# Copies of transposed q and k: reading PSUM in sequence and writing SBUF with a stride of three

## The chip, the cores and the metric

The kernel runs on one core of a Trainium2 chip. The metric is the device time of one execution in microseconds, as the median of several runs. Before the change it is 224.59 us (three runs, 224.47 to 225.51).

## The reference

Four batches with eight heads, 768 tokens and 64 columns per head go through attention in which each query sees the first 4 tokens and the last 128. The result, 3072 tokens of 512 columns, goes through a two-layer network with a swish of a beta per hidden column.

```python
scores = q @ k.T / sqrt(64)
keep = (pos[None, :] < 4) | ((rel >= 0) & (rel < 128))     # rel = query - key
a = softmax(where(keep, scores, -1e9))
x = (a @ v).reshape(3072, 512)
h = x @ w_in                                               # 512 -> 2048
out = (h * sigmoid(beta * h)) @ w_out                      # 2048 -> 512
```

## The kernel before, in words

Attention is cut into 32 units (`place`, L431): a unit `n` is a batch, a pair of heads and one half (384 tokens) of the sequence. Its q and k are loaded, cast to bf16 on GpSimd (L508; one on VectorE) and turned, so that the head's columns lie on the partitions: `qkT[pb]` holds, for each half, 384 columns of q and 384 of k. The scores (L560, L587, L624, L660) read `qkT` as both operands of TensorE's matmuls. Exponentials run on ScalarE (L563, L594, L631, L672), masks on VectorE (L605, L680) unless TensorE added them to the scores (L579), the product with v on TensorE (L703, L714), the division on VectorE (L723, L725). The result is turned back into `xT` (L742 and the copy L746, or a DMA). The network takes `xT` in eight stretches of 384 tokens: 16 groups of four matmuls with `w_in` (`hidden`, L765), a tanh on ScalarE (L773), a gate on VectorE (L788), and matmuls with `w_out` (`project`, L815) whose results leave through ScalarE and DMA.

Units 0 to 11 are turned by TensorE in `transpose_in` (L522); units 12 to 31 are turned by a DMA (L515), which the change doesn't touch. For the first twelve, the loads (`load_qk`, L444) put token 3p + c of the half onto partition p as its c-th piece, so that each descriptor covers three tokens. TensorE turns the three pieces c = 0, 1, 2 of q and of k one after the other into one bank of PSUM (L531): there the columns lie in the order (c, p), with c outside. `qkT` wants the tokens in their own order 3p + c, that is (p, c), with c inside. The copy from PSUM to `qkT` (`copy`, L536 to L541) puts them in order on its way.

The copies of units 2, 5, 6, 7, 8, 10 and 11 are one VectorE instruction over 768 elements, those of units 4 and 9 one of ScalarE (the table `TURN_IN`). Units 0, 1 and 3 are split into q on VectorE and k on ScalarE, 384 elements each, from two banks. That makes fifteen copies: seven and three on VectorE, two and three on ScalarE.

The order of work on each engine is fixed when the program is built: `Prog.order` (L178 on) places the operations by the cost that each is given and by their dependences, and `emit` writes one stream per engine with semaphore waits where another engine, or a VectorE or ScalarE result on the same engine, is needed. Each engine works through its stream strictly in order. The cost that `copy` gives the planner (L541) depends on the number of elements alone.

The start of the program runs units 0 to 3 one after the other, with filler matmuls on TensorE (`keep_busy`, L875). From then on TensorE alternates between `hidden` and `project` matmuls and the steps of later units, which the tables `EARLY` and `FIRST` put into slots.

The functions that the diff touches and what calls them:

Of the kernel before, what the change touches and what calls it, by code (L numbers as in the profile page):

```python
# [4 lines left out]
BF16 = mybir.dt.bfloat16  # L5
# [12 lines left out]
TT = 384  # L18
# [72 lines left out]
class Prog:  # L91
# [39 lines left out]
    def op(self, eng, fn, r=(), w=(), x=(), dma=None, busy=100.0, lag=None, behind=None,  # L131
           give=0.0, line=False, after=None):
        if self.group is not None and self.group.eng == eng:
            node = self.group
        else:
            node = Node(len(self.nodes), eng)
            self.nodes.append(node)
        events = []
        if after is not None:
            node.preds[after.id] = after  # L140
        if line:
            if self.line is not None:
                node.preds[self.line.id] = self.line
                self.line.soft.add(node.id)
            self.line = node

        def dep(ev, raw):
            if ev is None or ev[0] is node:
                return
            same = ev[0].eng == eng and ev[0].dma is None and dma is None  # L150
            node.preds[ev[0].id] = ev[0]
            if not same or (raw and eng != "pe"):
                events.append(ev)

        for t in r:
            dep(self.writer.get(t), True)
        for t in (*w, *x):
            dep(self.writer.get(t), False)
            for ev in self.readers.get(t, ()):
                dep(ev, False)  # L160
        if behind is not None:
            events.append((node, behind))
        me = (node, len(node.items))
        if dma is not None:
            self.dma_count[dma] = self.dma_count.get(dma, 0) + 16
            node.dma = (dma, self.dma_count[dma])
        node.items.append((fn, dma, events))
        node.busy += busy
        node.give = give
        node.lag = busy if lag is None else lag  # L170
        for t in r:
            self.readers.setdefault(t, []).append(me)
        for t in (*w, *x):
            self.writer[t] = me
            self.readers[t] = []
        return node
# [121 lines left out]
def bass_streamingllm_window__then__act_swish_beta_kernel(  # L298
# [21 lines left out]
    def sb(name, shape, dtype):  # L320
        ctx.append(nc.sbuf_tensor(name, list(shape), dtype))
        return ctx[-1].__enter__()
# [29 lines left out]
    qkT = [sb(f"qkT{z}", (128, 2, 2, TT), BF16) for z in range(4)]  # L352
# [17 lines left out]
    def pe(n):  # L370
        return {"busy": 2.5 + n / 2.4, "lag": 260.0}

    def act(n):
        return {"busy": 80.0 + 0.81 * n, "lag": 140.0}

    def dve(t):
        return {"busy": t, "lag": 140.0}
# [53 lines left out]
    def place(n):  # L431

        return n // 8, n % 4, n // 4 % 2, n % 4
# [88 lines left out]
    def transpose_in(n, bank=tr_ps, name_of="tr", eng="dve", apart=None):  # L522
        _, _, half, pb = place(n)
        z = n % NQK
        banks = [(bank, name_of, eng), apart or (bank, name_of, eng)]
        for which, name in enumerate("qk"):
            to, tag, _ = banks[which]
            with P.together("pe"):
                for c in range(3):
                    at = (3 * which + c) * 128  # L530
                    turned = op("pe", lambda e, which=which, c=c, at=at, to=to: nc.tensor.transpose(  # L531
                        to[:, :].bitcast(BF16)[:, at:at + 128],
                        qk16[z][:, which, c, :, :].rearrange("p h d -> p (h d)"), ident[:, :]),
                       r=[(name + "16", z), "ident"], w=[tag], **pe(128))

        def copy(eng, first, last, bank, tag, w):  # L536
            n = last - first
            dst = qkT[pb][:, half, first:last, :].rearrange("x w (p c) -> x w p c", c=3)
            src = bank[:, :].bitcast(BF16)[:, first * TT:last * TT].rearrange("x (w c p) -> x w p c", w=n, c=3)
            op(eng, lambda e: (e.copy if eng == "act" else e.tensor_copy)(dst, src), x=[tag], w=w,  # L540
               **(act(n * TT) if eng == "act" else dve(65.0 + n * 400.0)))  # L541

        if apart is None:
            copy(eng, 0, 2, bank, name_of, [("qT", pb, half), ("qkT", pb, half)])
        else:
            copy(eng, 0, 1, bank, name_of, [("qT", pb, half)])
            copy(apart[2], 1, 2, apart[0], apart[1], [("qkT", pb, half)])
        return turned
# [295 lines left out]
    for n in range(2, 4):  # L844
# [3 lines left out]
       w=["beta_stage"], dma="beta")  # L848
# [49 lines left out]
    for n in range(4):  # L898
# [19 lines left out]
       x=["acc0"], w=["beta"])  # L918
# [16 lines left out]
    for s in sorted(slots):  # L935
# [14 lines left out]
        for n, step in here:  # L950
            half = place(n)[2]
# [25 lines left out]
        if s in casts:  # L977
            n = casts[s]
# [20 lines left out]
        if s == 34:  # L999

            first = {0: (mask_a[:, :], MASK_A), 1: (mask_b[:, 128:512], MASK_B)}
# [78 lines left out]
```

## Time and profile before

| | |
|---|---|
| median of three runs | 224.59 us |
| the profiled execution | 225.3 us |
| its span, first to last instruction | 223.6 us |
| TensorE matmul busy | 217.0 us (97%) |
| VectorE busy | 128.9 us (58%), 257 instructions |
| ScalarE busy | 143.4 us (64%), 226 instructions |
| GpSimd busy | 72.1 us (32%) |
| first and last start of the changed copies | 5.3 and 52.7 us |

In the lines of the profile PE is TensorE's matmuls, PEld its weight loads, DVE VectorE, ACT ScalarE, POOL GpSimd and SP SyncE, with a q behind the name for the engine's own queue of instructions. L540 is line 540 of the kernel. Of a group of instructions the line shows its tiles, shapes and count, then total busy microseconds and mean nanoseconds of one, then the idle time of its engine ahead of it and what ended that. Tiles are named without their buffer numbers: `six` is the six banks of PSUM for scores and hidden columns, `acc` the two other banks. The ends of matmuls are modelled, so a full PE row doesn't mean that no matmul waited.

### The profile page before, as it was taken

To read this page: it belongs to the slowest core of one execution; us is meant where nothing else is said; L and a number is where in the kernel's file an instruction comes from. 1 tells how busy PE (TensorE), PEld (TensorE's weight loads), DVE (VectorE), ACT (ScalarE), POOL (GpSimd) and SP (SyncE) were. 2 spreads that over 40 slices of the span, in tenths; PEclk is the share of its full clock that TensorE was granted. 3 is DMA by queue.
4 is the path that set the end of the run, shared out by engine and by line. 5 is a ranking of instruction groups with operands and counts; after the bars stand their busy time and mean duration, and the time that the engine had idled before them with its cause. 6 is when DMAs were issued, how large, how long until landed. Compare 5 with 4: busy or idle time off the path is not lost.

```text
span 223.6 us, 4498 instructions
## 1 busy us (share of the span) xinstructions
PE 217.0 (97%) x1736; PEld 121.9 (55%) x1757; DVE 128.9 (58%) x257; ACT 143.4 (64%) x226; POOL 72.1 (32%) x149
## 2 busy tenths in 40 slices
PE   7998999999999999999999999999999999999995
PEld 4554556555545556555465556564656555555443
DVE  5474778898733367467194458574938466253300
ACT  2777996896256477666497568596767594465411
POOL 7666658987442213462210614600000000000000
PEclk9999999999999999999999999999999999999999
DMA  6999999997789999997995999622020202111022
GB/s 192 292 326 317 339 326 248 364 385 182 170 181 200 250 256 207 268 214 183 256 240 132 229 283 196 129 85 82 18 67 3 82 10 73 47 50 47 14 83 94
DMA packets 95437, 39.79 MB, mean 178 GB/s; under 512 B 81960, under 2 KB 88376, under 8 KB 95416
## 3 DMA queue, kind: packets, MB, share of 16 engines
q1 hardware_dynamic: 93760, 38.68, 68.1%
q10 hardware_dynamic: 1656, 0.83, 1.3%
q8 instruction: 14, 0.23, 0.5%
q14 instruction: 7, 0.06, 0.1%
HBM read 27.30 MB, written 6.29 MB: 150 GB/s over the span
## 4 chain that ended last, share of the span: by engine, by line
PE 86%; SPq 3%; DVE 2%; issue 2%; ACT 2%; POOL 2%; DMA 2%; POOLq 0%; DVEq 0%
PE acc L815 34%; PE six L765 31%; PE acc L765 5%; PE six L714 4%; PE six L660 3%; PE six L815 2%; SPq L457 2%; DMA v_stage<-in_v_dram 2%; PE six L587 1%; SPq L449 1%; PE six L703 1%; PE acc L796 1%; PE six L531 1%; PE six L560 1%; ACT th L773 1%
## 5 line engine op out<-in xcount | busy, mean ns | idle before, releaser
L815 PE MATMUL acc<-w_out,g 128*128 128x512 bf16 x332 | 84.0, 379 | 1.0 <-issue 0.3
L773 ACT ACTIVATE th<-six,beta_half 128x384 f32<-128x384 f32 x106 | 60.6, 583 | 30.0 <-PE six L765 24.1
L765 PE MATMUL six<-xT,w_in 128*128 128x384 bf16 x424 | 79.5, 326 | 0.1
L788 DVE SCALAR_TENSOR_TENSOR g<-th,six 128x384 bf16<-128x384 f32 x106 | 56.6, 550 | 26.5 <-ACT th L773 24.8
L765 PEld LDWEIGHTS six<-xT,w_in 128*128 128x128 bf16 x424 | 40.6, 98 | 29.9 <-issue 0.6
L815 PEld LDWEIGHTS acc<-w_out,g 128*128 128x128 bf16 x352 | 32.7, 98 | 33.7 <-issue 1.8
L680 DVE TENSOR_TENSOR E<-E,mask_all 128x1536 bf16<-128x1536 bf16 x20 | 19.4, 970 | 36.0 <-ACT E L672 26.6
L672 ACT ACTIVATE E<-six 128x1536 bf16<-128x1536 f32 x16 | 22.3, 1448 | 12.1 <-PE six L660 12.0
L508 POOL CAST qk<-q_stage 128x384 bf16<-128x384 f32 x32 | 16.5, 518 | 25.5 <-DMA q_stage<-in_q_dram 13.5
L511 POOL CAST v_aug<-v_stage 128x384 bf16<-128x384 f32 x32 | 17.1, 545 | 23.4 <-DMA v_stage<-in_v_dram 11.2
L594 ACT ACTIVATE E<-six 128x768 bf16<-128x768 f32 x24 | 19.3, 818 | 5.8 <-PE six L587 5.8
L508 POOL CAST qk<-k_stage 128x384 bf16<-128x384 f32 x31 | 17.3, 559 | 13.0 <-DMA k_stage<-in_k_dram 13.0
L823 ACT ACTIVATE out_sb<-acc 128x512 f32<-128x512 f32 x22 | 13.0, 595 | 10.5 <-PE acc L815 10.3
L765 PE MATMUL acc<-xT,w_in 128*128 128x384 bf16 x88 | 18.5, 327 | 0.7 <-DVE g L788 0.5
L714 PE MATMUL six<-v_aug,E 128*128 128x65 bf16 x384 | 19.0, 193 | 0.1
L714 PEld LDWEIGHTS six<-v_aug,E 128*128 128x128 bf16 x384 | 17.0, 97 | 3.6 <-issue 0.3
L725 DVE TENSOR_TENSOR o_norm<-six,rden 128x384 bf16<-128x384 f32 x32 | 17.8, 556 | 1.2
L788 DVE SCALAR_TENSOR_TENSOR g<-th,acc 128x384 bf16<-128x384 f32 x22 | 11.7, 548 | 5.0 <-ACT th L773 4.9
L773 ACT ACTIVATE th<-acc,beta_half 128x384 f32<-128x384 f32 x22 | 12.7, 591 | 2.6 <-PE acc L765 2.4
L563 ACT ACTIVATE E_sink<-six 128x384 bf16<-128x384 f32 x16 | 7.9, 497 | 5.7 <-PE six L560 5.7
L765 PEld LDWEIGHTS acc<-xT,w_in 128*128 128x128 bf16 x88 | 7.4, 98 | 5.6 <-DVE g L788 1.2
L703 PE MATMUL six<-v_sink,E_sink 128*128 128x130 bf16 x48 | 9.2, 220 | 0.1
(74 smaller groups left out, 155.6 us busy)
## 6 DMA issues: line engine op xcount, KB each, us to landing
out_dram<-out_sb SPq DMA_DIRECT2D x23, 256.0 KB, 2.6
wst<-in_moe_w_in_dram SPq DMA_DIRECT2D x8, 512.0 KB, 6.6
wst<-in_moe_w_out_dram SPq DMA_DIRECT2D x8, 512.0 KB, 8.5
q_stage<-in_q_dram SPq DMA_DIRECT2D x8, 384.0 KB, 3.7
k_stage<-in_k_dram SPq DMA_DIRECT2D x8, 384.0 KB, 4.0
v_stage<-in_v_dram SPq DMA_DIRECT2D x8, 384.0 KB, 4.4
v_stage<-in_v_dram SPq DMA_DIRECT2D x30, 96.0 KB, 4.7
q_stage<-in_q_dram SPq DMA_DIRECT2D x12, 192.0 KB, 5.3
```

Of the source, the lines that this page charges most:

```text
L508: op(eng, lambda e, x=x, name=name: e.tensor_copy(qk16[z][:, x, :, :, :], view(name)), r=[(name + "_stage", pb, half, hh) for hh in range( ...
L511: op("gp", lambda e: e.tensor_copy(v_aug[pb][:, 3 * half:3 * half + 3, :, 0:D], view("v")), r=[("v_stage", pb, half, hh) for hh in range(2 ...
L594: op("act", lambda e: e.activation(E[n % 2][:, c, :, 0:at], bank[:, 0:2, 0:at], AF.Exp, bias=0.0, scale=SCALE), x=[f"{name}0", f"{name}1"] ...
L672: op("act", lambda e, u=u, first=first: e.activation(E[u % 2][:, :, :, :].rearrange("p c h x -> p (c h x)"), six[:, first:first + 3, :].re ...
L680: op("dve", lambda e: e.tensor_tensor(both, both, mask_all[:, half, :].unsqueeze(1).to_broadcast([128, 2, 768]), ALU.mult), r=[("E", z, 0) ...
L714: last=(x == len(kbs) - 1): e.matmul(av_ps[:, at + hh * D1:at + hh * D1 + D1], E[z][:, c, h2, col:col + 128], v_aug[pb][:, kb, hh, :], sta ...
L725: op("dve", lambda e: e.tensor_tensor(o_norm[o][:, :, :, :].rearrange("p m h d -> p (m h) d"), src[:, :, 0:D], rden[z][:, :].unsqueeze(2). ...
L765: return op("pe", lambda e: e.matmul(bank, w_in16[:, c, m * 128:(m + 1) * 128], xT[:, c, T * TT:(T + 1) * TT], start=(c == 0), stop=(c == 3)),
L773: op("act", lambda e: e.activation(th[i % 3][:, :], bank, AF.Tanh, bias=0.0, scale=beta_half[:, m:m + 1]), x=[name], r=["beta"], w=[("th", ...
L788: op("dve", lambda e: e.scalar_tensor_tensor(g[T % 2][:, m, :], th[i % 3][:, :], 1.0, bank, ALU.add, ALU.mult), r=[("th", i % 3)], x=[name ...
L815: node = op("pe", lambda e: e.matmul(bank, g[T % 2][:, m, t * 128:(t + 1) * 128], w_out16[:, m, :], start=(m == 0), stop=(m == NM - 1)), r ...
L823: op("act", lambda e: e.activation(out_sb[z][:, :], bank, AF.Copy, bias=0.0, scale=0.5), x=[name], w=[("out_sb", z)], **act(NOUT))
```

## The change

The two views of the copy are built in another order of their dimensions. Before, both walk w (q, k), then p, then c: the write into `qkT` goes through memory in sequence, and the read from PSUM steps 128 elements (256 bytes) in its inner loop of three. After, both walk w, then c, then p: the read goes through PSUM in sequence, and the write steps three elements (6 bytes) in its inner loop of 128. The same elements land in the same places.

```diff
         def copy(eng, first, last, bank, tag, w):
             n = last - first
-            dst = qkT[pb][:, half, first:last, :].rearrange("x w (p c) -> x w p c", c=3)
-            src = bank[:, :].bitcast(BF16)[:, first * TT:last * TT].rearrange("x (w c p) -> x w p c", w=n, c=3)
+            dst = qkT[pb][:, half, first:last, :].rearrange("x w (p c) -> x w c p", c=3)
+            src = bank[:, :].bitcast(BF16)[:, first * TT:last * TT].rearrange("x (w c p) -> x w c p", w=n, c=3)
             op(eng, lambda e: (e.copy if eng == "act" else e.tensor_copy)(dst, src), x=[tag], w=w,
                **(act(n * TT) if eng == "act" else dve(65.0 + n * 400.0)))
```

## The prediction

> **What bounds the kernel now.** I read the chain that ended last first, then the stages, then the groups that hold the changed line, then each copy's surroundings in the timeline. The page gives the frame:
>
> ```profile
> span 223.6 us, 4498 instructions
> PE 86%; SPq 3%; DVE 2%; issue 2%; ACT 2%; POOL 2%; DMA 2%; POOLq 0%; DVEq 0%
> ```
>
> The stages (columns: time, then busy time and count of PE, PEld, DVE, ACT and POOL, granted clock, DMA share, GB/s) show where that chain is not PE:
>
> ```profile
> 4.00:18.00 14.00, 13.53 (x145) 7.81 (x143) 8.24 (x18) 8.75 (x14) 9.88 (x21) 1.00 1.07 313
> 18.00:36.00 18.00, 17.07 (x169) 9.45 (x170) 13.02 (x26) 15.84 (x29) 12.01 (x21) 1.00 1.04 317
> 36.00:56.00 20.00, 19.95 (x179) 11.62 (x178) 17.67 (x36) 16.30 (x29) 16.72 (x28) 1.00 0.94 298
> 56.00:223.60 167.60, 163.78 (x1237) 91.42 (x1255) 87.77 (x169) 101.07 (x153) 30.61 (x66) 1.00 0.61 138
> ```
>
> The clock is 1.00 throughout. TensorE, which works strictly in its written order, is nearly gapless from 18 us to the end, so microseconds that it loses early aren't won back: they come out at the end. All fifteen copies of the changed line lie in the first 54 us, the start (before 18 us) and the stretch in which VectorE and ScalarE are busy for 72% to 88% of the time. So the question is what one copy costs after the change, and which copies TensorE waits for.
>
> **The change part by part.** Nothing is added or moved: the same fifteen instructions on the same engines, with the same costs given to the planner, so the same order, waits and DMAs. What changes is the walk of each copy. Before, its inner loop reads PSUM at every 128th element (256 bytes) and writes SBUF in sequence; after, it reads in sequence and writes at every third element (6 bytes).
>
> Cost of a copy now, beside the copy L746, which is in sequence on both sides:
>
> ```profile
> L540 DVE COPY qkT<-six 128x768 bf16<-128x768 bf16 x7 | 6.7, 953 | 1.4 <-PE six L531 1.4
> L540 ACT COPY qkT<-six 128x768 bf16<-128x768 bf16 x2 | 1.6, 799 | 0.4 <-PE six L531 0.4
> L540 DVE COPY qkT<-acc 128x384 bf16<-128x384 bf16 x2 | 1.1, 558 | 1.4 <-PE acc L531 1.4
> L540 ACT COPY qkT<-six 128x384 bf16<-128x384 bf16 x2 | 1.0, 479 | 0.0
> L746 DVE COPY xT<-six 128x384 bf16<-128x384 bf16 x7 | 2.5, 353 | 1.9 <-PE six L742 1.9
> L746 ACT COPY xT<-six 128x384 bf16<-128x384 bf16 x2 | 1.0, 476 | 0.1
> ```
>
> VectorE: (953 - 558) / 384 = 1.03 ns an element, with 163 ns fixed. ScalarE: (799 - 479) / 384 = 0.83 ns, with 159 fixed. The ScalarE copy in sequence costs 476 against 479, so ScalarE pays nothing for the strided reads and has nothing to win. The VectorE copy in sequence takes 353: less the same 163 that is 190 / 384 = 0.49 ns, twice the rate. So there are 205 ns in a 384 copy and some 400 in a 768 copy to be won if a strided write, unlike a strided read, left the double rate in place.
>
> [...]
>
> I take no gain: the doubled row is the only one with both sides in sequence, and after the change the write side is as broken as the read side was.
>
> Is there a loss from the strided write? No copy of the trace has it. The nearest rows are VectorE's fills, two of which write one 2-byte element every 65 or 130 elements:
>
> ```profile
> L388 DVE MEMSET v_sink<- 128x1040 f32 x1 | 0.9, 925 | 0.1
> L388 DVE MEMSET ones<- 128x256 bf16 x1 | 0.3, 272 | 0.0
> L388 DVE MEMSET v_aug<- 128x12 bf16 x4 | 0.2, 68 | 0.0
> L388 DVE MEMSET v_sink<- 4x16 bf16 x2 | 0.1, 72 | 0.2
> L388 DVE MEMSET ones<- 32x32 f32 x1 | 0.1, 85 | 0.9 <-PEq L1062 0.9
> ```
>
> The three fills in sequence lie on a line: (925 - 272) / 784 and (272 - 85) / 224 are both 0.83 ns an element, with 58 fixed. It gives 58 + 12 × 0.83 = 68 for v_aug and 58 + 16 × 0.83 = 71 for v_sink; measured 68 and 72. Half a cycle more per element would have shown as 6 to 8 ns. So scattered 2-byte writes cost nothing visible there. The weakness: the runs are short, and the steps are 130 and 260 bytes, not 6, where neighbours fall into the same few words. The ends for the unknown price are therefore: below, the doubled rate (-400 ns for 768 elements, -205 for 384); above, one more cycle for every element, that is the rate halved as the row of L746 shows it doubled (+790 on VectorE and, at 0.83 ns, +640 on ScalarE for 768; half for 384). I take **zero**, by the fills.
>
> Next, what each copy is worth. Call d the growth of a VectorE copy of 768 and a that of ScalarE's; a copy of 384 grows by half. The timeline (start, duration, engine, and in brackets the idle time before it with what ended it):
>
> ```profile
> 11.25 0.10 PEld L587 LDWEIGHTS six<-qkT 64*128 64x128 bf16 x2 [0.29 <-DVE qkT L540]
> 18.14 0.50 PE L765 MATMUL acc<-xT,w_in 128*128 128x384 bf16 x2 [0.19 <-POOL w_in L493]
> 19.34 0.80 ACT L540 COPY qkT<-six 128x768 bf16<-128x768 bf16 x1 [0.40 <-PE six L531]
> 20.19 0.11 PEld L587 LDWEIGHTS six<-qkT 64*128 64x128 bf16 x4 [0.63 <-ACT qkT L540]
> 21.60 0.95 DVE L540 COPY qkT<-six 128x768 bf16<-128x768 bf16 x1
> 22.33 0.11 PEld L587 LDWEIGHTS six<-qkT 64*128 64x128 bf16 x4 [0.32 <-issue]
> 24.84 1.02 DVE L788 SCALAR_TENSOR_TENSOR g<-th,acc 128x384 bf16<-128x384 f32 x2 [1.37 <-ACT th L773]
> 27.35 0.54 DVE L788 SCALAR_TENSOR_TENSOR g<-th,acc 128x384 bf16<-128x384 f32 x1
> 28.01 0.11 PEld L587 LDWEIGHTS six<-qkT 64*128 64x128 bf16 x4 [0.32 <-DVE g L788]
> 29.65 0.96 DVE L540 COPY qkT<-six 128x768 bf16<-128x768 bf16 x1 [0.34 <-PE six L531]
> 34.78 1.09 PEld L765 LDWEIGHTS acc<-xT,w_in 128*128 128x128 bf16 x8 [0.37 <-DVE g L788]
> 39.45 0.96 DVE L540 COPY qkT<-six 128x768 bf16<-128x768 bf16 x1 [0.47 <-PE six L531]
> 40.64 0.10 PEld L587 LDWEIGHTS six<-qkT 64*128 64x128 bf16 x2 [0.32 <-DVE qkT L540]
> 46.54 0.60 ACT L773 ACTIVATE th<-acc,beta_half 128x384 f32<-128x384 f32 x1
> 47.29 0.10 PEld L587 LDWEIGHTS six<-qkT 64*128 64x128 bf16 x2 [0.32 <-ACT th L773]
> 55.46 0.36 DVE L746 COPY xT<-six 128x384 bf16<-128x384 bf16 x1 [0.59 <-PE six L742]
> ```
>
> - Units 0 to 3: k of units 0 and 1 on ScalarE and the whole of unit 2 (scores at 11.25 start when it ends) pass their growth along TensorE's start: a/2 + a/2 + d. But at 18.14 TensorE stands 0.19 us for a weight cast on GpSimd, which covers that much. q of units 0, 1 and 3 runs beside the other engine's copy.
> - Unit 4 (ScalarE, 19.34 to 20.14): the scores start 0.05 us later, so a passes whole.
> - Unit 5 (21.60): VectorE has 1.37 us to spare before 24.84; nothing passes.
> - Unit 6: the copy delays the gate at 27.35 to 27.89, and with it the scores at 28.01. The same 0.32 of idle also stands before scores that wait for nothing (22.33), so it is no wait for the copy: a released start takes 0.05, and 0.07 is to spare. d - 0.07 passes.
> - Unit 7 (29.65) begins VectorE's fullest stretch, whose end TensorE waits for at 34.78. d passes.
> - Unit 8 ends at 40.41, scores at 40.64: d - 0.18.
> - Unit 9 (ScalarE) delays the tanh that ends at 47.14, scores at 47.29: a - 0.10.
> - Units 10 and 11: VectorE has 0.59 to spare at 55.46: 2d - 0.59 if that is above zero.
>
> With d = a = 0 the sum is 0.0: the forecast is the median, **224.6 us** (the profiled execution took 225.3 for its span of 223.6; the sum is a difference, so it moves either figure alike, and I give it on the median of 224.59).
>
> **The rivals.**
>
> *Slower: the strided write costs part of a cycle for each element.* [...] d = 0.5 × 1.03 × 768 = 0.40, a = 0.32. Sum: start 0.16 + 0.16 + 0.40 - 0.19 = 0.53; unit 4 0.32; unit 6 0.33; unit 7 0.40; unit 8 0.22; unit 9 0.22; units 10 and 11 0.21; together 2.2: **226.8**. A whole cycle gives 1.24 + 0.64 + 0.72 + 0.79 + 0.61 + 0.54 + 0.99 = 5.5: 230.1. From a third of a cycle (d 0.26, a 0.21: 0.29 + 0.21 + 0.19 + 0.26 + 0.08 + 0.11 = 1.1) it leaves the half per cent. For it: no row shows steps this small. Against it: the fills, and the freedom from cost of the strided reads.
>
> [...]
>
> *Faster: reading PSUM in sequence is enough for the double rate on VectorE.* d = -0.40. TensorE then gains only where it truly stood for VectorE: 0.37 at 34.78; the start's gain ends at the weight cast of 18.14, and units 6 and 8 end in the fixed 0.32. That is **224.2**; were all three of units 6, 7 and 8 worth their 0.40, 1.2 and 223.4. For it: the row of L746. Against it: both of its sides are in sequence.
>
> *Nothing changes because the walk is the same to the engine.* The copies would show the same durations for another reason; same time as the forecast, counted with it.
>
> **How the numbers follow.** This kernel's three runs span 224.47 to 225.51, so about 0.5% (1.1 us) is what a measurement can tell from no change. Rates unchanged: 0.46, with a range of its own of 224.1 to 225.2. Strided write dearer: 0.45, of which 0.03 below a third of a cycle. Double rate: 0.09, of which 0.06 beyond half a per cent. So faster 0.06, same 0.46 + 0.03 + 0.03 = 0.52, slower 0.42. The range goes from 223.4, the best of the faster case, to 229.0, which takes in the dearer write up to about 0.8 of a cycle (d 0.63, a 0.51: 0.95 + 0.51 + 0.56 + 0.63 + 0.45 + 0.41 + 0.67 = 4.2, and as much as 0.2 for a slack that I saw too large); what is left out, a whole cycle, has under 0.1.
>
> **What would show it.** Right: VectorE's copies at 953 and 558 and ScalarE's at 799 and 479, within 10 ns. The slower rival: VectorE's 768 at 1.2 us or more, scores at 11, 20 and 40 us starting later, and TensorE from 56 us on moved as a whole. The faster one: 550. A split, with ScalarE dearer and VectorE not, would move units 4 and 9 alone. The step most open to error is the price of a write at a 6-byte step, taken from fills with far steps; the next is that time lost before 18 us is partly covered.

## The result, and the profile after

The changed kernel takes 227.69 us (227.53 to 227.85, four runs) against 224.57 (224.47 to 225.51): 1.0129 of the time before, with a 95% interval of 1.0101 to 1.0158. That is 3.1 us more; the two profiled spans differ by 2.5 (226.1 and 223.6). A second measurement gave 227.69 against 225.26: 1.0104 (1.0079 to 1.0129). Both intervals lie above 1, so the change makes the kernel slower. Of the runs below, one execution, the profiled one of the first run with VectorE alone, took 784 us; it stands outside the ratio, and its trace isn't read.

The frame of the page (it counts 21 instructions more since the trace of before lacks the records of 21 matmuls of L815; the programs have the same), and the groups of the changed line with two that were not changed:

```profile
span 226.1 us, 4519 instructions
PE 87%; DVE 8%; ACT 3%; issue 0%; DVEq 0%
```

```profile
L540 DVE COPY qkT<-six 128x768 bf16<-128x768 bf16 x7 | 10.1, 1446 | 1.4 <-PE six L531 1.4
L540 ACT COPY qkT<-six 128x768 bf16<-128x768 bf16 x2 | 2.9, 1457 | 0.8 <-PE six L531 0.8
L540 DVE COPY qkT<-acc 128x384 bf16<-128x384 bf16 x2 | 1.6, 800 | 1.6 <-PE acc L531 1.6
L540 ACT COPY qkT<-six 128x384 bf16<-128x384 bf16 x2 | 1.6, 812 | 0.0
L746 DVE COPY xT<-six 128x384 bf16<-128x384 bf16 x7 | 2.5, 354 | 1.4 <-PE six L742 1.4
L388 DVE MEMSET v_aug<- 128x12 bf16 x4 | 0.2, 68 | 0.0
```

All fifteen copies grew: VectorE's from 953 to 1446 ns and from 558 to 800, ScalarE's from 799 to 1457 and from 479 to 812, while L746, in sequence on both sides, stands at 354 (353 before), and the scattered fills of v_aug at 68. Per element VectorE now takes (1446 - 800) / 384 = 1.68 ns and ScalarE (1457 - 812) / 384 = 1.68: two engines with different rates before (1.03 and 0.83) have the same rate after. In the chain, VectorE's share went from 2% to 8%.

The stages after (same columns as before):

```profile
4.00:18.00 14.00, 12.87 (x139) 7.43 (x138) 8.56 (x17) 9.62 (x14) 10.25 (x21) 1.00 1.08 315
18.00:36.00 18.00, 16.68 (x169) 9.06 (x167) 13.16 (x24) 15.83 (x28) 13.32 (x23) 1.00 1.06 335
36.00:56.00 20.00, 19.11 (x171) 11.35 (x171) 18.62 (x34) 16.22 (x29) 16.14 (x27) 1.00 0.93 293
```

In these three stages, 52 us, PE's busy time fell by 0.66 + 0.39 + 0.84 = 1.9 us: TensorE stood that much longer. From 56 us on the work is only moved (the table of scores below). The copies and the waits behind them in the timeline:

```profile
12.15 0.10 PEld L587 LDWEIGHTS six<-qkT 64*128 64x128 bf16 x2 [0.78 <-DVE qkT L540]
19.87 1.44 ACT L540 COPY qkT<-six 128x768 bf16<-128x768 bf16 x1 [0.81 <-PE six L531]
21.36 0.11 PEld L587 LDWEIGHTS six<-qkT 64*128 64x128 bf16 x4 [1.26 <-ACT qkT L540]
29.16 0.11 PEld L587 LDWEIGHTS six<-qkT 64*128 64x128 bf16 x4 [0.32 <-DVE qkT L540]
33.97 1.53 DVE L605 TENSOR_TENSOR E<-E,mask_b 128x768 bf16<-128x768 bf16 x2
36.01 1.09 PEld L765 LDWEIGHTS acc<-xT,w_in 128*128 128x128 bf16 x8 [0.15 <-DVE g L788]
42.19 0.10 PEld L587 LDWEIGHTS six<-qkT 64*128 64x128 bf16 x2 [0.63 <-DVE qkT L540]
49.18 0.10 PEld L587 LDWEIGHTS six<-qkT 64*128 64x128 bf16 x2 [0.32 <-ACT qkT L540]
54.66 0.34 PEld L531 LDWEIGHTS six<-ident,qk 128*128 128x128 bf16 x6 [0.97 <-DVE qkT L540]
```

Against before, the scores at 12.15 (11.25) are 0.9 us late, those at 21.36 (20.19) 1.2, those at 42.19 (40.64) 1.6, those at 49.18 (47.29) 1.9. (How much of this a second trace of the same kernel would show is asked below.) The last line is new: unit 11's transposes stand 0.97 us for the copy of unit 10. Before, the same transposes waited for nothing, and the scores behind them started 2.5 us earlier than the 55.10 of after; VectorE's masks stand with them for a comparison below:

```profile
32.40 1.86 DVE L605 TENSOR_TENSOR E<-E,mask_b 128x768 bf16<-128x768 bf16 x2
51.92 0.54 PEld L531 LDWEIGHTS six<-ident,qk 128*128 128x128 bf16 x6
52.56 0.10 PEld L587 LDWEIGHTS six<-qkT 64*128 64x128 bf16 x2
```

### The profile page after: what moved, and what is told of

Read it like the earlier page. It is cut to its first block, busy times and chain, and to the rows that moved or that the text cites. A ratio compares the mean times of both kernels' runs of the same rounds, so it can differ in the third digit from the quotient of the medians.

```text
span 226.1 us, 4519 instructions
## 1 busy us (share of the span) xinstructions
PE 219.0 (97%) x1757; PEld 121.7 (54%) x1757; DVE 132.8 (59%) x257; ACT 145.2 (64%) x226; POOL 72.9 (32%) x149
## 4 chain that ended last, share of the span: by engine, by line
PE 87%; DVE 8%; ACT 3%; issue 0%; DVEq 0%
PE acc L815 34%; PE six L765 28%; PE six L714 5%; PE acc L765 3%; DVE qkT L540 3%; PE six L660 3%; DVE g L788 3%; PE six L579 2%; PE six L587 2%; PE six L815 2%; DVE E L605 1%; ACT E L594 1%; PE six L560 1%; PE six L531 1%; PE six L703 1%; PE acc L875 1%
## 5 line engine op out<-in xcount | busy, mean ns | idle before, releaser
L815 PE MATMUL acc<-w_out,g 128*128 128x512 bf16 x352 | 88.5, 379 | 0.0
L815 PEld LDWEIGHTS acc<-w_out,g 128*128 128x128 bf16 x352 | 32.7, 98 | 33.7 <-issue 1.8
L508 POOL CAST qk<-q_stage 128x384 bf16<-128x384 f32 x32 | 17.0, 533 | 29.4 <-DMA q_stage<-in_q_dram 14.9
L511 POOL CAST v_aug<-v_stage 128x384 bf16<-128x384 f32 x32 | 17.7, 565 | 25.8 <-DMA v_stage<-in_v_dram 12.6
L508 POOL CAST qk<-k_stage 128x384 bf16<-128x384 f32 x31 | 15.6, 506 | 11.9 <-DMA k_stage<-in_k_dram 11.7
L540 DVE COPY qkT<-six 128x768 bf16<-128x768 bf16 (+1 forms) x8 | 10.9, 1366 | 1.9 <-PE six L531 1.9
```

The lines of the kernel that those rows point to most:

```text
L508: op(eng, lambda e, x=x, name=name: e.tensor_copy(qk16[z][:, x, :, :, :], view(name)), r=[(name + "_stage", pb, half, hh) for hh in range( ...
L511: op("gp", lambda e: e.tensor_copy(v_aug[pb][:, 3 * half:3 * half + 3, :, 0:D], view("v")), r=[("v_stage", pb, half, hh) for hh in range(2 ...
L815: node = op("pe", lambda e: e.matmul(bank, g[T % 2][:, m, t * 128:(t + 1) * 128], w_out16[:, m, :], start=(m == 0), stop=(m == NM - 1)), r ...
```

## Experiments

Ratios are to runs of before on the same chip. Where a kernel has the copies in both forms, the two walks stand behind a condition:

```diff
+            walk = "x w c p" if <condition> else "x w p c"
-            dst = ...rearrange("x w (p c) -> x w p c", c=3)
-            src = ...rearrange("x (w c p) -> x w p c", w=n, c=3)
+            dst = ...rearrange("x w (p c) -> " + walk, c=3)
+            src = ...rearrange("x (w c p) -> " + walk, w=n, c=3)
```

### What a strided write costs: the first probe

Single copies and fills behind the last work of the kernel of before. The diff is a summary: in the kernel each is a line of its own, and a dozen more (short runs, 32-bit copies of ScalarE, strided reads of SBUF) are left out here.

```diff
+    for s in (1, 2, 3, 4, 6, 8, 12, 16, 32):      # 16-bit, hb: a bank of PSUM; fx: SBUF
+        e.tensor_copy(fx[:, 0:384 * s:s], hb[:, 0:384])
+    for s in (1, 2, 3, 4, 16):                    # 32-bit
+        e.tensor_copy(fx32[:, 0:384 * s:s], h32[:, 0:384])
+    e.tensor_copy(fx[:, 0:1152].rearrange("p (a b) -> p a b", b=6)[:, :, 0:2], ...)
+    for n, s in ((384, 1), (384, 3), (12, 65), (188, 65)):
+        e.memset(fx[:, 0:n * s:s], 0.0)
+    for s in (1, 2, 3, 4, 8, 16):                 # ScalarE, 16-bit
+        e.copy(fw[:, 0:384 * s:s], ab[:, 0:384])
```

> The kernel of before with some forty single copies and fills put behind its last work, PSUM to SBUF, 128 partitions, each with another step of the write; their results are used by nothing, so the time of the whole means nothing and only the durations count. Theory A (an element that is written with a step of over one word costs a second slot of about 0.83 ns, whatever the engine and the step): 16-bit copies of 384 at 558 (VectorE, step 1 at 353 in pairs) and at 803 for every step from 3 up, ScalarE 479 and 805; a fill of 384 at step 3 slower than at step 1 by 320 ns, the fill of 188 at step 65 by 157, and short runs of 12 hardly. Theory B (only steps that keep neighbours in the same few words cost; far steps are free, as the fills at steps 65 and 130 seemed to show): 803 at steps 2 to 4, back to 558 at steps of 16 and 32, and the fill at step 65 at 58 + 188 x 0.83 = 214 ns. Theory C (the engine's walk over three encoded dimensions costs, not the step): a single run at step 3 takes 558, as none of these copies has a second dimension.

VectorE, in the timeline: 16-bit steps 1, 2, 3, 4, 6, 8 and 32, then 32-bit steps 3, 4 and 16, then 192 pairs of adjacent 16-bit elements every 6 elements, then two 16-bit fills, 384 at step 3 and 188 at step 65:

```profile
211.68 0.36 DVE L1052 COPY xT<-six 128x384 bf16<-128x384 bf16 x1
212.07 0.59 DVE L1053 COPY xT<-six 128x384 bf16<-128x384 bf16 x1
212.69 0.80 DVE L1054 COPY xT<-six 128x384 bf16<-128x384 bf16 x1
213.53 1.01 DVE L1055 COPY xT<-six 128x384 bf16<-128x384 bf16 x1
214.58 1.45 DVE L1056 COPY xT<-six 128x384 bf16<-128x384 bf16 x1
216.06 1.88 DVE L1057 COPY xT<-six 128x384 bf16<-128x384 bf16 x1
221.67 1.82 DVE L1060 COPY xT<-six 128x384 bf16<-128x384 bf16 x1
226.61 0.66 DVE L1067 COPY xT<-six 128x384 f32<-128x384 f32 x1
227.30 0.84 DVE L1068 COPY xT<-six 128x384 f32<-128x384 f32 x1
228.17 0.81 DVE L1069 COPY xT<-six 128x384 f32<-128x384 f32 x1
229.01 0.41 DVE L1070 COPY xT<-six 128x384 bf16<-128x384 bf16 x1
230.54 0.38 DVE L1073 MEMSET xT<- 128x384 bf16 x1 [0.39 <-DVE xT L1072]
231.85 0.21 DVE L1075 MEMSET xT<- 128x188 bf16 x1 [0.75 <-DVE xT L1074]
```

ScalarE, 16-bit steps 1, 3 and 8:

```profile
224.61 0.48 ACT L1077 COPY w_in<-acc 128x384 bf16<-128x384 bf16 x1 [6.65 <-DVE acc L1051]
225.74 0.80 ACT L1079 COPY w_in<-acc 128x384 bf16<-128x384 bf16 x1
228.35 1.87 ACT L1081 COPY w_in<-acc 128x384 bf16<-128x384 bf16 x1
```

None of the three theories holds. The cost isn't one extra slot (A): it grows with the step. It isn't confined to near steps (B): it grows up to step 8 and then stays. And it isn't the encoded shape (C): single runs pay. Less the 0.16 us fixed, an element takes 1.12, 1.67, 2.21, 3.36 and 4.48 ns at steps 2, 3, 4, 6 and 8, and 4.3 at 32. A step of 8 elements is 16 bytes, and 4.48 times 2/8, 3/8, 4/8 and 6/8 is 1.12, 1.68, 2.24 and 3.36. So the times are those of about 4.5 ns for each 16-byte line that the copy writes in pieces, on either engine (ScalarE takes 1.67 ns an element at step 3 and 4.45 at step 8); at step 3 that is 1.68 ns an element, the rate of the changed copies. On VectorE, 32-bit elements at steps of 3, 4 and 16 take 1.30, 1.77 and 1.69, about 1.75 for a line: less than half. The pairs come to (0.41 - 0.16) / 192 = 1.30 a pair, the price of a 32-bit element at the same 12 bytes. The fills pay nothing: 384 at step 3 take 0.38, which is 58 + 384 × 0.83 = 377 ns.

### Which side of it is slow: the second probe

Seven of its eighteen copies, fills and products:

```diff
+    e.tensor_copy(fx[:, 0:1152:3], fx[:, 4000:4384])                        # from SBUF
+    e.tensor_copy(fx[:, 0:1152:3], h32[:, 0:384])                           # fp32 to 16 bits
+    e.tensor_scalar(fx32[:, 0:1152:3], h32[:, 0:384], 0.5, None, ALU.mult)  # fp32 to fp32
+    e.tensor_tensor(fx[:, 0:1152:3], fx[:, 4000:4384], fx[:, 5000:5384], ALU.mult)
+    e.memset(fx[:, 0:3072:8], 1.0)
+    e.copy(fw[:, 0:1152:3], fw[:, 4000:4384])                               # ScalarE, from SBUF
+    e.copy(fw32[:, 0:1152:3], ab[:, 0:384])                                 # ScalarE, 16 bits to fp32
```

> Single copies and fills behind the last work of the kernel of before, as in the first probe, whose result was: 16-bit copies pay by 16-byte lines (4.4 to 4.5 ns for each line that they touch, from step 2 to step 8, and flat beyond), 32-bit copies 1.7 ns for a line, fills nothing. Theory (an element of half a 4-byte word costs extra when it is written alone, whatever the source): 384 elements at step 3 take 0.80 from SBUF, from fp32 and with a multiplication too, at step 8 1.9; a 32-bit write of 16-bit sources at step 3 takes 0.66; fills of ones at step 8 0.38 like fills of zeros. Rival (it is the way from PSUM that is slow): from SBUF 0.56. Rival (it is the 16-bit source): from fp32 0.66. Rival for the fills (zeros are a special case): ones at step 8 1.8.

In the order of the diff:

```profile
213.30 0.49 DVE L1052 COPY xT<-xT 128x384 bf16<-128x384 bf16 x1
214.89 0.80 DVE L1054 CAST xT<-six 128x384 bf16<-128x384 f32 x1
216.56 0.68 DVE L1056 TENSOR_SCALAR xT<-six 128x384 f32<-128x384 f32 x1
217.27 0.80 DVE L1057 TENSOR_TENSOR xT<-xT 128x384 bf16<-128x384 bf16 x1
221.76 0.38 DVE L1060 MEMSET xT<- 128x384 bf16 x1 [1.46 <-issue]
224.40 0.83 ACT L1066 COPY w_in<-w_in 128x384 bf16<-128x384 bf16 x1 [4.81 <-DVE acc L1051]
228.74 0.66 ACT L1069 CAST w_in<-acc 128x384 f32<-128x384 bf16 x1 [0.46 <-ACT out_sb L802]
```

The product of two SBUF tensors, written at step 3, takes 0.80 like the copy from PSUM, and ScalarE from SBUF 0.83: the source doesn't matter. Nor does its type: fp32 to 16 bits 0.80, 16 bits to fp32 0.66. What counts in these runs is the size of the element that is written alone. VectorE's copy within SBUF is the exception: 0.49 at step 3 and, in the same trace, 1.02 at step 8. Less the 0.16 fixed these are 0.86 and 2.24 ns an element, half the price at both steps; why is open. Fills of ones at step 8 are as free as those of zeros (0.38 both); why fills are spared wasn't found.

### The parts: VectorE alone, ScalarE alone, and the whole again

Conditions `eng == "dve"` and `eng == "act"`.

> Only the ten VectorE copies write with the step of three; the five ScalarE copies stay as before; the order of work is that of before. Theory (the strided write costs each engine on its own account, and the end moves through the scores that wait): VectorE's copies at 1446 and 803 ns, ScalarE's at 799 and 479, and by the prediction's sum with d = 0.49 and a = 0: start 0.49 - 0.19 = 0.30, unit 6 0.42, unit 7 0.49, unit 8 0.31, units 10 and 11 0.39: 1.9 us above before. Rival (ScalarE's copies carry the loss, since its growth per copy is the larger): under 0.8 us. Rival (each loss is hidden unless the other is there too): under 0.8 us here and in the next run.

> Only the five ScalarE copies write with the step of three. Theory: ScalarE's copies at 1457 and 805 ns, VectorE's at 953 and 558, and by the prediction's sum with a = 0.66 and d = 0: start 0.33 + 0.33 - 0.19 = 0.47, unit 4 0.66, unit 9 0.56: 1.7 us above before; together with the run before it 3.6, where the full change showed 3.1. Rival (VectorE carries all of it): under 0.5 us.

> The whole change once more, so that it and its parts stand beside the same runs of before on one chip. Theory: between 1.0% and 1.6% above before (2.3 to 3.5 us), with VectorE's copies at 1.44 and 0.80 us and ScalarE's at 1.46 and 0.81. Rival (the first measurement was a chance of its chip): about 0.75%, the sum of its two parts as measured (0.54% and 0.21%).

> Only the VectorE copies, again, since the trace of the first run of this part can't be read. Theory, mended by the run with ScalarE alone (whose delay from unit 4 vanished under VectorE's full stretch before 34.8 us): the two parts don't add up, because each engine's delay is covered while the other engine is the late one; VectorE alone 1.2 us (0.54%) as before, with most of it behind unit 7: from 30 to 41 us the scores late by 0.5 to 0.9, at 55 us by 1.2 to 1.6. Rival (the parts add up): 1.9 us.

Measured: VectorE alone 1.0054 (1.0034 to 1.0074) and, again, 1.0058 (1.0021 to 1.0096); ScalarE alone 1.0021 (0.9999 to 1.0043); the whole 1.0104 (1.0079 to 1.0129). With VectorE alone the scores are 0.75 late at 41.39 and 1.4 at 53.99, as expected. In microseconds the parts and the whole are 1.2 to 1.3, 0.5 and 2.3, where the sum had 1.9, 1.7 and 3.8: each part is smaller than its terms, ScalarE's by most. 0.58% and 0.21% make 0.79%, just the lower end of the whole's interval; whether the parts add up isn't settled.

The expectation of the second run with VectorE alone says that ScalarE's delay from unit 4 vanishes under VectorE's full stretch before 34.8 us. The traces don't show that. With ScalarE alone, unit 4's scores are 0.55 late (20.74 for 20.19), and those of unit 8 only 0.10 (40.74 for 40.64). But VectorE's two masks in between, the first of these lines, are 0.34 shorter than the 1.86 of before, and the same two masks are as short in the second line, from the run with units 10 and 11 alone, whose copies up to there are those of before:

```profile
32.84 1.52 DVE L606 TENSOR_TENSOR E<-E,mask_b 128x768 bf16<-128x768 bf16 x2
32.14 1.53 DVE L608 TENSOR_TENSOR E<-E,mask_b 128x768 bf16<-128x768 bf16 x2
```

With ScalarE alone the masks start 0.44 late and end 0.10 late. So the delay went in masks that differ from one execution to the next, and it is no cover that the change can count on. How much of ScalarE's delay reaches the end is known by the times alone: 0 to 1.0 us by the interval, where the sum had 1.7.

The starts of the weight loads of some scores in the traces:

| scores of | before | after | whole, again | VectorE alone | ScalarE alone | units 0-3 | units 10, 11 | all but 10 |
|---|---|---|---|---|---|---|---|---|
| unit 4 | 20.19 | 21.36 | 20.67 | 20.59 | 20.74 | 20.58 | 19.93 | 21.69 |
| unit 8 | 40.64 | 42.19 | 41.63 | 41.39 | 40.74 | 40.65 | 40.05 | 42.51 |
| unit 9 | 47.29 | 49.18 | 48.62 | 48.45 | 47.48 | 47.30 | 47.04 | 49.51 |
| unit 10 | 52.56 | 55.10 | 54.54 | 53.99 | 52.88 | 52.70 | 52.60 | 54.93 |
| units 16, 17 | 92.81 | 95.37 | 94.79 | 94.23 | 93.13 | 92.94 | 92.85 | 95.23 |

Each column is one execution, and the first rows vary from one to the next. The two probes run the work of before up to 200 us, so they are two more traces of it: their scores of unit 4 start at 20.02 and at 21.71, where before has 20.19. The first row by itself therefore shows no effect of a change. A step down a column varies less: from unit 4 to unit 8 the probes take 20.19 and 20.24, before 20.45, the whole change 20.83 and 20.96.

From unit 10 to units 16 and 17 every column takes 40.24 to 40.27, but for 40.30 in the last: what is lost by 55 us stays lost, and nothing is lost after it. From unit 9 to unit 10 it is 5.27 before (5.27 and 5.31 in the probes), 5.92 in both traces of the whole change, 5.54 with VectorE's copies alone and 5.40 with ScalarE's.

### Units 0 to 3, units 10 and 11, and all but unit 10

Conditions on the unit: `n < 4`, `n in (10, 11)`, `n != 10`.

> Only the copies of units 0 to 3 (four of VectorE, three of ScalarE) write with the step of three. The prediction's term: 0.33 + 0.33 + 0.49 - 0.19 = 0.96 us. Theory now: the scores of units 1 to 3 start 0.4 to 0.9 late as in the changed kernel, but the weights that come by DMA until 32 us, and VectorE's slack before 34.8, cover most: 0 to 0.4 us at the end. Rival (nothing covers): 0.9.

> Only the copies of units 10 and 11 (both VectorE, 768) write with the step of three. The prediction's term: 2 x 0.49 - 0.59 = 0.39 us, by VectorE's slack at 55.46. Theory from the changed kernel's trace: unit 11's transposes go into the bank that unit 10's copy reads, so they wait for it, and 0.3 to 0.7 us is lost there, before VectorE's slack counts at all; the wait of the transposes for the copy should show at 52 us. Rival (hidden): none.

> The whole change, but unit 10's copy as before (0.95 us). Theory: in the changed kernel TensorE stands about a microsecond before unit 11's transposes, for unit 10's copy to leave the bank; with that copy short the wait falls below 0.6 and the end is 0.3 to 0.5 us earlier than the whole change, so 0.85% above before where the whole change had 1.04%. Rival (VectorE's load behind it sets the time, as the prediction had it): the wait goes but the end stays.

Units 0 to 3: 1.0011 (0.9994 to 1.0028), 0.25 us and at most 0.6, where the term was 0.96. In its trace the scores of unit 3 are 0.75 late (15.06 for 14.31), those of unit 4 0.39, those of unit 8 0.01. So most of what the first units lose doesn't reach the end. Where it is given back isn't shown: the masks at 32 us took 1.43 here and 1.86 before, and the time from unit 3's scores to unit 4's is 5.52, as with units 10 and 11 alone, where nothing up to there is changed.

Units 10 and 11: 1.0017 (0.9993 to 1.0042), 0.4 us, no more than the edge of the measurement; the trace has 0.29 from unit 9 to unit 10 (5.56 against 5.27). The wait of the transposes shows, but not all of it comes from the longer copy: with ScalarE alone and with units 0 to 3 alone, where unit 10's copy is as before, the same transposes stand 0.44 and 0.13 is lost.

```profile
52.16 0.34 PEld L531 LDWEIGHTS six<-ident,qk 128*128 128x128 bf16 x6 [0.60 <-DVE qkT L543]
```

All but unit 10: 1.0081 (1.0050 to 1.0113) beside the whole's 1.0104; the times can't tell the two apart, the trace can. From unit 9 to unit 10 it takes 5.42 instead of 5.92, with the masks there as long as in the whole change, so half a microsecond of the whole change's loss is that one copy. Its wait has halved, not gone:

```profile
54.49 0.34 PEld L531 LDWEIGHTS six<-ident,qk 128*128 128x128 bf16 x6 [0.47 <-DVE qkT L543]
```

### Both sides in sequence

```diff
-            dst = ...rearrange("x w (p c) -> x w p c", c=3)
-            src = ...rearrange("x (w c p) -> x w p c", w=n, c=3)
+            dst = qkT[pb][:, half, first:last, :]
+            src = ...rearrange("x (w y) -> x w y", w=n)
```

> All fifteen copies read PSUM in sequence and write SBUF in sequence, so the columns of q and k stay in the order in which they were turned: the keys and queries are permuted against the masks, and only the time means something. Theory (the rate falls through the step of the written or read side, and VectorE has its double rate only where both are in sequence): VectorE's copies at 553 and 353 ns, ScalarE's unchanged at 799 and 479; the end gains 0.4 us (the one true wait at 34.78) to 1.2 us. Rival (before's copies are held by something else than the step): 953 and 558 ns and no gain.

0.9969 (0.9952 to 0.9987): 0.7 us gained, between the 0.4 and the 1.2. The rate is the doubled one:

```profile
L540 DVE COPY qkT<-six 128x768 bf16<-128x768 bf16 x7 | 3.9, 551 | 1.4 <-PE six L531 1.4
L540 DVE COPY qkT<-acc 128x384 bf16<-128x384 bf16 x2 | 0.7, 359 | 2.2 <-PE acc L531 2.2
```

### Two ways on: the true costs in the plan, and tokens in order

```diff
-  **(act(n * TT) if eng == "act" else dve(65.0 + n * 400.0))
+  **(act(n * TT * 2) if eng == "act" else dve(65.0 + n * 645.0))
```

> The whole change, with the copies' measured costs given to the planner (VectorE 65 + 645 per 384 elements, ScalarE twice its cost per element), so that the order of work is laid out anew around the longer copies. Theory (the loss is time on the path, not a bad order): at most a third of the loss comes back: 0.7% to 1.1% above before. Rival (the order was the loss): within 0.3% of before.

The second way, cut short (the old body of `load_qk` goes, and the copy is that of the run in sequence):

```diff
     def load_qk(n, name, queue="sp"):
+        for hh in range(2):
+            load_head(n, name, hh, queue)
```

> Units 0 to 11 load their q and k with tokens p, p + 128 and p + 256 on partition p, one DMA for each head as the later units do, so that TensorE turns them into their own order and both sides of every copy run in sequence; the planner lays out the order anew for the other loads. Copies as in the run in sequence (553 and 353 on VectorE), which gained 0.3%. Theory: runs of 256 bytes instead of 768 and twice as many DMAs cost the start, which waits for q, k and the weights, more than the copies give: 0.5 to 3 us above before. Rival (the DMAs have room): 0.3% below before.

The plan with the true costs took 1.0220 (1.0188 to 1.0252): twice the loss, outside what either theory gave. In this try the planner's order wasn't made better by a better price of one kind of work; which of its moves cost the time was not followed up. With the tokens in order the copies ran at 553 and 352 ns, but the kernel took 1.0385 (1.0342 to 1.0427), 8.7 us more, where 0.5 to 3 were expected. Its q and k loads beside those of before (count, KB each, us from issue to landing):

```profile
q_stage<-in_q_dram SPq DMA_DIRECT2D x32, 96.0 KB, 3.4
k_stage<-in_k_dram SPq DMA_DIRECT2D x28, 96.0 KB, 3.6
```

```profile
q_stage<-in_q_dram SPq DMA_DIRECT2D x12, 192.0 KB, 5.3
k_stage<-in_k_dram SPq DMA_DIRECT2D x10, 192.0 KB, 5.5
```

The pieces land no later than before, but SP issues 60 loads of q and k for them where it issued 38 (these 22, and 16 small ones that the later units have in both kernels), and each is about half a microsecond of its queue (mostly 0.49 in the chain that ended last, 0.46 the shortest): in this kernel's chain of waits SP's loads of single heads (q, k and v) hold 9.0% of the span, where before SP's queue held 3% in all. The new order that the planner laid out is in the time too. No version tried beats before with its work done in full.

## Why the prediction was right and wrong, step by step

**The price of the strided write failed: zero was taken, +493 ns on VectorE and +658 on ScalarE, for 768 elements, were measured.** The step was "I take zero, by the fills". The fills were read rightly, and the probe shows that they stay free with 384 elements at steps of 3 and 8 and with 188 at 65. They were the wrong proxy: a fill isn't a copy (at step 3, 384 elements take 0.38 us in a fill and 0.80 in a copy). The forecast of no change, 224.6, fell with this step; the measured 227.69 lies in the range, 223.4 to 229.0, only because the range was opened for the slower rival. The weakness that the prediction named (short runs, far steps) wasn't the one that broke it. Its other reason, that strided reads cost nothing, carried over to writes without a row. The rates after (1.68 ns on both engines) lie between the prediction's half and whole extra cycle on VectorE (1.55 and 2.06), and just above the whole one on ScalarE (1.66).

**The slower rival was the case that came, with other numbers.** It had half a cycle more for each element, and with it 226.8 us. No run shows that half cycle, 0.52 ns on VectorE and 0.42 on ScalarE: the copies of 768 grew by 0.64 ns an element on VectorE and 0.86 on ScalarE. The probes show a price by 16-byte lines, the same in nanoseconds on both engines, and over twice as high for 16-bit elements as for 32-bit ones (4.5 ns against 1.75). That the rival's 2.2 us comes near the 2.3 to 3.1 measured is in part luck: its prices (0.40 and 0.32) were too small, and the shares of them that it let through too large. At steps of 16 bytes and more a 32-bit element costs 1.77 and 1.69 ns here. With two or three 16-bit elements to a line (step 3), each already took 1.68 ns instead of 1.03.

**The sum, with the measured d = 0.49 and a = 0.66, gives 3.8 us; 2.3 to 3.1 were measured.** Term by term, from the growth of the lateness in the two traces of the changed kernel, against before's one:

| term | by the sum | in the trace | in the second trace |
|---|---|---|---|
| start, up to unit 4's copy, and unit 4 | 0.96 + 0.66 | 1.17 | 0.48 |
| unit 6 (scores at 28.01, then 29.16) | 0.42 | none | none |
| unit 7 (34.78, then 36.01) | 0.49 | 0.08 | 0.20 |
| unit 8 (40.64, then 42.19) | 0.31 | 0.32 | 0.32 |
| unit 9 (47.29, then 49.18) | 0.56 | 0.34 | 0.34 |
| units 10 and 11 (52.56, then 55.10) | 0.39 | 0.65 | 0.65 |

- The start: the cover of 0.19 at 18.14 was too small. Units 0 to 3 alone cost 0.25 us by the times, and at most 0.6, not 0.96. The traces can't place it, since the start varies by more than the term (20.02 to 21.71 without any change).
- Unit 6: I took the gate that the row named as what released the scores. After the change the gate ends later still and the scores are late by no more than those ahead of them, so it wasn't. The copy itself ended at 27.43, 0.53 before them once the 0.05 of a released start is taken off, and that covers d. I had seen that 0.32 of idle is the same before scores that wait for nothing, and then priced its named releaser all the same.
- Unit 7: here before's trace is the odd one. Its two masks took 1.86; in the probes and with units 10 and 11 alone, whose copies up to there are the same, they took 1.60, 1.64 and 1.53. From unit 6's scores to the weights behind the gate (34.78) these three take 6.51, 6.55 and 6.44, before 6.77, the changed kernel 6.85 and 6.97. Against the three, 0.3 to 0.5 of the 0.49 passed, so the term was nearer than the table says. The 0.37 for which TensorE stood there is 0.16 in one of the three and gone in the others: it was read from a single execution. The rows show the durations; what sets the length of the masks isn't shown. (GpSimd's cast of weights that began with before's masks, at 32.40, took 1.46; the one before it, and the last ones ahead of the masks in the changed kernel and with ScalarE alone, took 1.04.)
- Unit 9: most of its 0.34 isn't ScalarE's copy. That copy ended at 46.66, 0.58 before the scores once the 0.05 is taken off, so all but 0.08 of a was covered: the named releaser was priced again. With ScalarE alone the term is 0.09 (6.74 from unit 8's scores to unit 9's, for 6.65); with VectorE alone it is 0.41 (7.06). In that kernel TensorE stands, between the two, for a gate of VectorE that came in time before (first line). In the changed kernel too that gate is late, behind a mask that took 0.56 before (second line) and now begins 0.01 us behind a GpSimd cast of 1.04. The mask has 1.43 or 1.44 in all four traces in which unit 8's copy is longer (the whole change twice, all but unit 10, VectorE alone), so the change may well bring it there. But with units 10 and 11 alone, where that copy is as before, the next mask was nearly as long (third line) and the loss the same 0.34 (6.99), so that the change causes this term isn't shown:

```profile
45.97 0.44 PEld L766 LDWEIGHTS acc<-xT,w_in 128*128 128x128 bf16 x4 [0.35 <-DVE g L789]
44.81 1.43 DVE L605 TENSOR_TENSOR E<-E,mask_a 128x768 bf16<-128x768 bf16 x1
44.42 1.34 DVE L608 TENSOR_TENSOR E<-E,mask_b 128x768 bf16<-128x768 bf16 x1 [0.22 <-ACT E L597]
```

- Units 10 and 11: the prediction counted VectorE's slack at 55.46 and didn't ask who writes next into the bank that the copy reads. That wait came first, and unit 10's copy cost half a microsecond there. The rest of the 0.65 fits a third mask, ahead of that copy, which took 0.55 before; but it took 0.71 and 1.19 in the probes too, and there little was lost (5.27 and 5.31 from unit 9 to unit 10):

```profile
51.10 1.21 DVE L605 TENSOR_TENSOR E<-E,mask_a 128x768 bf16<-128x768 bf16 x1
```

**The rest held.** The order of work didn't change; lost time on TensorE before 56 us came out at the end in full (2.54 us at unit 10's scores, 2.5 between the two spans); reading in sequence alone gave no double rate (1446 ns), and both sides in sequence gave it (551 ns) and 0.7 us.

## What to carry to other kernels

When a rearrangement has to break one side of a copy, break the read: a strided read of PSUM took 1.03 ns an element on VectorE, where both sides in sequence took 0.50, and 0.83 on ScalarE, as in sequence (0.82), while a strided 16-bit write to SBUF cost up to 4.5 ns an element on both engines. If the write must be strided, write whole 4-byte words: every 12 bytes, a pair of 16-bit elements took VectorE 1.30 ns, a single one 3.36. In pricing a longer copy, ask not only who reads its result but who next writes the buffer that it reads, and check that an instruction named as a releaser did end just before. A trace is one execution: before a wait of 0.3 us is put into a sum, look for it in a second trace of the same work.

## What the runs showed of the hardware

A 16-byte line of SBUF that VectorE or ScalarE writes 16 bits at a time took about 4.5 ns (384 elements at step 8: 1.88 us on VectorE, 1.87 on ScalarE); 32 bits at a time about 1.75 (384 at step 4: 0.84 us and 0.83); two adjacent 16-bit elements that VectorE wrote every 12 bytes took 1.30 ns, as one 32-bit element at the same step did. Scattered fills took no more than the 58 ns and 0.83 ns an element of fills in sequence: 384 2-byte elements in 0.38 us, where a copy took 0.80 at step 3 and 1.88 at step 8. A copy within SBUF on VectorE took 0.49 at step 3 where the other 16-bit forms took 0.80 to 0.83. Two masks of VectorE, 128x768 each, took 1.86 us together in before's execution and 1.53 with units 10 and 11 alone, whose copies up to there are those of before.
